# Attention outputs transposed by a crossbar DMA instead of TensorE and VectorE, with the schedule around it shifted

## The chip, the cores and the metric

The kernel runs on one core of one Trainium2 chip. The metric is the time of one execution on the device in microseconds (us), as the median of several runs; most runs of one kernel agree within 0.3%. A profile of one execution gives a page and a trace. Engines are named as the profile names them: PE is TensorE, PEld its weight loads, DVE VectorE, ACT ScalarE, POOL GpSimd, SP the engine that only issues transfers here; SPq is its queue.

## The reference

Two operators follow one another. The first is attention with a hash mask: 4 batches, 8 heads, 768 positions, 64 values per head. A query sees a key only if the signs of six random projections of both agree. The second is a feed-forward block on the 3072 x 512 result: x times w_in (512 x 2048), SiLU, times w_out (2048 x 512).

```python
q_bits = (np.einsum('bhsd,dk->bhsk', q, proj) > 0)      # same for k; bits give a bucket
mask = q_bucket[:, :, :, None] == k_bucket[:, :, None, :]
scores = np.where(mask, scale * np.matmul(q, k.transpose(0, 1, 3, 2)), -1000000000.0)
attn = softmax(scores)                                   # cut
x = np.matmul(attn, v).transpose(0, 2, 1, 3).reshape(B * S, H * D)
h = x @ w_in
out = (h * (1.0 / (1.0 + np.exp(-h)))) @ w_out
```

## The kernel before

Heads are worked in pairs: 16 pairs, four to a batch. A head takes nine windows; a window has one 512-wide score tile (TensorE), its exponential (ScalarE) and four products with v (TensorE). One batch is a stage of 72 windows. While stage b runs, the second operator of batch b-1 is spread through its windows, in units of four 512-column matmuls (or eight of 256). Stage one has no such units; after the last window, the last batch's units run alone.

The attention result of a pair, `x_pr`, has positions on partitions; the first matmul of the second operator needs it transposed, `xT`. Before the change TensorE does it, and VectorE copies the result out of PSUM:

```python
    def x_unit(p):
        xp = ps.tile([P, S], F16, tag="m", name="xt_ps", bufs=3)
        for t in range(NJ):                      # NJ = 6
            nc.tensor.transpose(xp[:, t * P : (t + 1) * P], x_pr[p][:, t, :], ident16)
        xT[p] = xpl.tile([P, S], F16, tag=f"xT{p % 4}", name="xT")
        nc.vector.tensor_copy(out=xT[p], in_=xp)
```

Its first use, one unit of the second operator (four pairs are the four k-tiles, so all four transposes of a batch must be there before the fourth matmul of the first unit):

```python
            for j in range(f):
                ft = grp * f + j
                for dt in range(NDT):            # NDT = 4
                    nc.tensor.matmul(hp[:, j, :], w_in16[dt][:, ft * P : (ft + 1) * P],
                                     xT[4 * b + dt][:, c0 : c0 + n], ...)
```

Everything is placed by window number, and a queue executes in the order of placement. Almost all transfers are issued from one queue (SP), in order; of the large ones only the two weight matrices are loaded from GpSimd's queue, cast to two bytes on the way:

```python
    for dt in range(NDT):
        plan(12 + 6 * dt, lambda dt=dt: load_w_in(dt))
        plan(58 + 5 * dt, lambda dt=dt: load_w_out(dt))     # 4 x 512 KB
    ...
    for Q in range(2, NQUAD):                    # a quad is two pairs, 36 windows
        w0 = (Q - 1) * QST
        ...
            plan(w0 + 1 + i, lambda p=2 * Q + i: load_v(p))
            if Q + 1 < NQUAD:                    # eight loads of 96 KB per pair, 128 B packets
                plan(w0 + (12 if Q == 2 else 21) + i, lambda p=2 * Q + 2 + i: load_blocks(p))
    for p in range(NPAIR):
        plan(2 * NU * (p + 1) + (3 if p % 4 == 3 else 9), lambda p=p: x_unit(p))
    ...
        if w % BST == 1:
            moeq.extend(moe_head())              # units left over by the batch before
        if w % BST == 5 and w > BST:
            moeq.extend(moe_list(w // BST - 1))  # units of the batch that has just ended
```

The softmax here doesn't subtract the row's maximum and nothing guards it: scores larger than these inputs give would overflow.

Of the kernel before, what the change touches and what calls it, by code (L numbers as in the profile page):

```python
# [10 lines left out]
F16 = mybir.dt.float16  # L11
# [6 lines left out]
def kernel(  # L18
# [10 lines left out]
    nc = tc.nc  # L29
    B, H, S, D = q.shape  # L30
# [3 lines left out]
    P = 128  # L34
    NJ = S // P
    NDT = DMODEL // P
    NFT = DFF // P
# [9 lines left out]
    cst = ctx.enter_context(tc.tile_pool(name="cst", bufs=1))  # L47
# [8 lines left out]
    gpl = ctx.enter_context(tc.tile_pool(name="gpl", bufs=1))  # L56
    ops = ctx.enter_context(tc.tile_pool(name="ops", bufs=3))
    ps = ctx.enter_context(tc.tile_pool(name="ps", bufs=1, space=bass.MemoryType.PSUM))
# [31 lines left out]
    def load_v(p):  # L90
        b, h0 = p // 4, 2 * (p % 4)
        t = vld.tile([P, 2, NJ * D], F32, tag="ldv", name="v_sb")
        nc.sync.dma_start(
            out=t, in_=v[b, h0 : h0 + 2].rearrange("h (p t) d -> p h (t d)", p=P))
        v_sb[p] = t
# [18 lines left out]
    ident = cst.tile([P, P], F32, name="ident")  # L114
# [2 lines left out]
    nc.vector.memset(pw, 0.0)  # L117
    nc.gpsimd.dma_start(out=pw[0:64, 0:NBIT], in_=proj)
    nc.gpsimd.dma_start(out=pw[64:128, NBIT + 1 : 2 * NBIT + 1], in_=proj)
    ident16 = cst.tile([P, P], F16, name="ident16")  # L120
    nc.vector.tensor_copy(out=ident16, in_=ident)



# [60 lines left out]
    def block_unit(p, n):  # L185
        if n == 0:
            qk32[p] = t32.tile([P, 2 * S], F32, tag="qk32", name="qk32")

        dst = qk32[p][:, n * S : (n + 1) * S].rearrange(
            "p (t r a) -> p a t r", t=NJ, r=32, a=4)  # L190
        nc.vector.transpose(out=dst, in_=qk_sb[p, "qk"[n]])  # L191
# [96 lines left out]
    NU = 9  # L288
# [24 lines left out]
    x_pr = {}  # L313
# [48 lines left out]
    xT = {}  # L362

    def x_unit(p):
        xp = ps.tile([P, S], F16, tag="m", name="xt_ps", bufs=3)
        for t in range(NJ):
            nc.tensor.transpose(xp[:, t * P : (t + 1) * P], x_pr[p][:, t, :], ident16)  # L367
        xT[p] = xpl.tile([P, S], F16, tag=f"xT{p % 4}", name="xT")
        nc.vector.tensor_copy(out=xT[p], in_=xp)


    after = []
# [1 line left out]
    def flush():  # L374
        for fn in after:
            fn()
        after.clear()

    def moe_units(b):
        g = {}  # L380

        def mm1(ci, grp):
            c0, n, f = ((0, 512, 1), (512, 256, 2))[ci]
            if grp == 0:
                g[ci] = gpl.tile([P, NFT, n], F16, tag=f"g{ci}", name="g")
            hp = ps.tile([P, f, n], F32, tag="m", name="h_ps", bufs=3)
            for j in range(f):
                ft = grp * f + j
                for dt in range(NDT):
                    nc.tensor.matmul(hp[:, j, :], w_in16[dt][:, ft * P : (ft + 1) * P],  # L390
                                     xT[4 * b + dt][:, c0 : c0 + n],
                                     start=(dt == 0), stop=(dt == NDT - 1))
            th = thp.tile([P, f, n], F32, tag="th", name="th")
            nc.scalar.activation(out=th, in_=hp, func=AF.Tanh, scale=0.5)  # L394

            after.append(lambda: nc.vector.scalar_tensor_tensor(  # L396
                out=g[ci][:, grp * f : (grp + 1) * f, :], in0=th, scalar=1.0, in1=hp,
                op0=ALU.add, op1=ALU.mult))

        o2 = {}  # L400

        def mm2_last():

            for i in range(2):
                c = slice(i * DMODEL // 2, (i + 1) * DMODEL // 2)
                op = ps.tile([P, DMODEL // 2], F32, tag="s", name="o2_ps", bufs=3)
                for ft in range(NFT):
                    nc.tensor.matmul(op, g[1][:, ft, P : 2 * P], w_out16[:, ft, c],  # L408
                                     start=(ft == 0), stop=(ft == NFT - 1))
                osb = ops.tile([P, DMODEL // 2], F32, tag="osb", name="osb")  # L410
                nc.vector.tensor_scalar(out=osb, in0=op, scalar1=0.5, scalar2=None,
                                        op0=ALU.mult)
                dst = out[b * S : (b + 1) * S, c].rearrange("(p t) n -> p t n", p=P)
                nc.sync.dma_start(out=dst[:, NJ - 1, :], in_=osb)

        def mm2(tt, part):
            ci, ct = (0, tt) if tt < 4 else (1, tt - 4)
            if part == 0:
                tag = "m" if scoring else "s"
                o2[tt] = ps.tile([P, DMODEL], F32, tag=tag, name="o2_ps", bufs=3)  # L420
            for ft in range(4 * part, 4 * part + 4):
                nc.tensor.matmul(o2[tt], g[ci][:, ft, ct * P : (ct + 1) * P],  # L422
                                 w_out16[:, ft, :],
                                 start=(ft == 0), stop=(ft == NFT - 1))
            if part == 3:
                osb = ops.tile([P, DMODEL], F32, tag="osb", name="osb")
                nc.vector.tensor_scalar(out=osb, in0=o2[tt], scalar1=0.5, scalar2=None,  # L427
                                        op0=ALU.mult)
                dst = out[b * S : (b + 1) * S, :].rearrange("(p t) n -> p t n", p=P)
                nc.sync.dma_start(out=dst[:, tt, :], in_=osb)  # L430

        first = [lambda grp=grp: mm1(0, grp) for grp in range(NFT)]
        second = [lambda grp=grp: mm1(1, grp) for grp in range(NFT // 2)]
        outs = {tt: [lambda tt=tt, part=part: mm2(tt, part) for part in range(4)]
                for tt in range(NJ)}
        if b == B - 1:
            outs[NJ - 1] = [mm2_last]
        return first, second, outs

    def spread(x, y):  # L440

        both = [((i + 0.5) / len(x), 0, u) for i, u in enumerate(x)]
        both += [((i + 0.5) / len(y), 1, u) for i, u in enumerate(y)]
        return [u for _, _, u in sorted(both, key=lambda e: e[:2])]

    late = []

    def moe_head():
        units, late[:4] = late[:4], []
        return units  # L450

    def moe_list(b):


        first, second, outs = moe_units(b)
        units = spread(first, late) + spread(second, sum((outs[t] for t in range(4)), []))
        late[:] = outs[4] + outs[5]
        return units


# [2 lines left out]
    BST = 8 * NU  # L463
    QST = 4 * NU
# [13 lines left out]
    def plan(w, fn):  # L478
        at.setdefault(w, []).append(fn)
# [34 lines left out]
    for Q in range(2, NQUAD):  # L514
        w0 = (Q - 1) * QST
        for i in range(4 if Q > 2 else 0):
            w1 = w0 + (5, 9, 11, 14)[i]
            plan(w1, lambda Q=Q, i=i: block_unit(2 * Q + i // 2, i % 2))
            if i % 2:
                for par in range(2):  # L520
                    plan(w1, lambda p=2 * Q + i // 2, par=par: cast_unit(p, par))
        plan(w0 + 20, lambda Q=Q: proj_unit(2 * Q, 2 * Q + 1))
        for i in range(4):
            plan(w0 + 20,
                 lambda Q=Q, i=i: bits_unit((2 * Q, 2 * Q + 1), i // 2, i % 2))
        for i in range(2):
            plan(w0 + 1 + i, lambda p=2 * Q + i: load_v(p))
            for j in range(2):
                plan(w0 + 18 + 9 * i + 2 * j, lambda p=2 * Q + i, j=j: v_unit(p, (j,)))
            if Q + 1 < NQUAD:  # L530
                plan(w0 + (12 if Q == 2 else 21) + i, lambda p=2 * Q + 2 + i: load_blocks(p))
    for p in range(NPAIR):
        plan(2 * NU * (p + 1) + (3 if p % 4 == 3 else 9),
             lambda p=p: x_unit(p))

    moeq = deque()
# [3 lines left out]
    for w in range(NW):  # L540
        flush()
        for fn in at.pop(w, []):
            fn()
        if w % BST == 1:
            moeq.extend(moe_head())
        if w % BST == 5 and w > BST:
            moeq.extend(moe_list(w // BST - 1))
        keep = 3 if w >= NW - 12 else 0
        left = BST - w % BST
        n = -(-(len(moeq) - keep) // left) if len(moeq) > keep else 0  # L550
        if n == 1 and len(moeq) - keep < left and (w % 3 == 2 or w % QST in (20, 21)):
            n = 0
        for _ in range(n):
            moeq.popleft()()
        av(w)
        if w + LEAD < NW:
            score(w + LEAD)
# [7 lines left out]
    for u in moe_head() + moe_list(B - 1) + late:  # L565
        u()
        flush()
# [28 lines left out]
```

## Time and profile before

| | before |
|---|---|
| time, median of 3 runs | 315.19 us (315.08 to 315.35) |
| span of the profiled run | 313.6 us |
| PE / DVE / ACT busy | 97% / 60% / 68% of the span |
| granted TensorE clock | 1.0 |

The page is read from the chain of waits (its section 4): what ended last, followed back, says which engine sets the end. A group's line (section 5) has busy time and mean length of one, then the idle time of its engine just before it and what ended most of that. A mean length of a matmul is not its price: they overlap, and the price is the distance from start to start.

### The profile page before, as it was taken

What the parts mean: (1) busy time and instruction counts of PE and PEld (TensorE: products, weight loads), DVE (VectorE), ACT (ScalarE), POOL (GpSimd) and SP (SyncE); (2) the same over time, 40 slices, a digit from 0 to 9 for tenths busy, and PEclk for the clock granted to TensorE, in tenths of its full rate; (3) what the DMA queues carried; (4) which work ended last, traced back from release to release, by engine and by line L of the source; (5) the groups of instructions that cost most, each with busy time, mean ns of one, the idle gap of its engine ahead of it and who ended that gap; (6) DMA issues with size and microseconds to landing.
All of it is one profiled execution on the core that took longest, in us unless ns stands there. A gap on an engine that the chain in (4) does not pass through costs nothing.

```text
span 313.6 us, 7308 instructions
## 1 busy us (share of the span) xinstructions
PE 305.5 (97%) x2795; PEld 180.9 (58%) x2795; DVE 186.7 (60%) x372; ACT 212.1 (68%) x389; POOL 124.6 (40%) x197
## 2 busy tenths in 40 slices
PE   6999999999999999999999999999999999999995
PEld 3566665555666565545566566545566665446554
DVE  4788968696559524774658444685533434664341
ACT  2897989998876576878877666786876761553210
POOL 6477999567514831374505750174511110000000
PEclk9999999999999999999999999999999999999999
DMA  7999997980584028800791158500000000001112
GB/s 176 240 254 235 216 148 112 234 139 8 92 136 142 9 45 131 234 7 9 118 201 54 40 81 147 182 2 9 4 36 33 36 33 36 34 0 54 49 58 79
DMA packets 92564, 30.22 MB, mean 96 GB/s; under 512 B 82432, under 2 KB 89072, under 8 KB 92528
## 3 DMA queue, kind: packets, MB, share of 16 engines
q1 hardware_dynamic: 89776, 25.54, 36.9%
q0 software_dynamic: 2752, 4.20, 8.0%
q8 instruction: 22, 0.36, 0.5%
q14 instruction: 14, 0.11, 0.1%
HBM read 27.27 MB, written 6.29 MB: 107 GB/s over the span
## 4 chain that ended last, share of the span: by engine, by line
PE 87%; DVE 6%; ACT 3%; DMA 2%; issue 1%; SPq 0%; ACTq 0%
PE h_ps L390 26%; PE o_ps L422 25%; PE s_ps L306 17%; PE o_ps L338 11%; PE bp_ps L232 3%; ACT u L309 2%; PE tp_ps L177 2%; DMA k_sb<-in_k_dram 2%; PE xt_ps L367 2%; DVE g L396 1%; PE o_ps L408 1%; DVE qk L191 1%; DVE qkb L283 1%; DVE qka L283 1%; DVE qka L255 1%
## 5 line engine op out<-in xcount | busy, mean ns | idle before, releaser
L309 ACT ACTIVATE u<-s_ps 128x512 f16<-128x512 f32 x288 | 156.9, 601 | 45.3 <-PE s_ps L306 44.8
L396 DVE SCALAR_TENSOR_TENSOR g<-th,h_ps 128x512 f16<-128x512 f32 x96 | 65.4, 685 | 84.7 <-ACT th L394 84.5
L390 PE MATMUL h_ps<-xT,win 128*128 128x512 f16 (+1 forms) x512 | 97.1, 326 | 0.6 <-DVE g L396 0.6
L422 PE MATMUL o_ps<-wout,g 128*128 128x512 f16 x368 | 92.2, 379 | 0.0
L338 PEld LDWEIGHTS <-u 128*128 128x128 f16 x1152 | 68.2, 98 | 41.5 <-ACT u L309 9.4
L394 ACT ACTIVATE th<-h_ps 128x512 f32<-128x512 f32 x96 | 57.3, 597 | 39.0 <-PE h_ps L390 36.2
L338 PE MATMUL o_ps<-vv,u 128*128 128x65 f16 x1152 | 82.6, 194 | 0.5
L390 PEld LDWEIGHTS <-win 128*128 128x128 f16 x512 | 49.9, 98 | 32.6 <-issue 1.6
L358 POOL TENSOR_TENSOR x_pr<-osum,rec 128x384 f16<-128x384 f32 x21 | 17.3, 825 | 97.6 <-DVE rec L357 97.2
L422 PEld LDWEIGHTS <-g 128*128 128x128 f16 x368 | 35.4, 98 | 32.6
L306 PE MATMUL s_ps<-qka 71*128 71x512 f16 x192 | 52.7, 327 | 0.6 <-DVE qka L255 0.6
L306 PE MATMUL s_ps<-qkb 128*128 128x512 f16 x192 | 52.7, 326 | 0.0
L199 POOL TENSOR_SCALAR qka<-qk 64x1536 f16<-64x1536 f32 x15 | 21.9, 1463 | 20.0 <-DVE qk L191 12.8
L199 POOL TENSOR_SCALAR qkb<-qk 64x1536 f16<-64x1536 f32 x15 | 22.0, 1468 | 1.2
L427 DVE TENSOR_SCALAR osb<-o_ps 128x512 f32<-128x512 f32 x23 | 15.8, 687 | 9.4 <-PE o_ps L422 9.4
L210 POOL TENSOR_TENSOR vsa<-v_sb 128x192 f32<-128x192 f32 x32 | 19.3, 602 | 0.0
L208 POOL CAST vv<-v_sb 128x384 f16<-128x384 f32 x32 | 16.4, 513 | 3.0 <-DMA v_sb<-in_v_dram 2.8
L306 PEld LDWEIGHTS <-qka 71*128 71x128 f16 x192 | 15.5, 97 | 1.2 <-issue 1.0
L191 DVE STREAM_TRANSPOSE qk<-q_blk 128x768 f32<-128x768 f32 x10 | 15.7, 1573 | 0.0
L191 DVE STREAM_TRANSPOSE qk<-k_blk 128x768 f32<-128x768 f32 x10 | 15.7, 1571 | 0.0
L306 PEld LDWEIGHTS <-qkb 128*128 128x128 f16 x192 | 15.4, 97 | 0.0
L352 DVE TENSOR_TENSOR osum<-o_ps,vsum 128x390 f32<-128x390 f32 x21 | 11.9, 566 | 1.8
(57 smaller groups left out, 184.8 us busy)
## 6 DMA issues: line engine op xcount, KB each, us to landing
v_sb<-in_v_dram SPq DMA_DIRECT2D x16, 384.0 KB
out_dram<-osb SPq DMA_DIRECT2D x23, 256.0 KB
q_blk<-in_q_dram SPq DMA_DIRECT2D x40, 96.0 KB
k_blk<-in_k_dram SPq DMA_DIRECT2D x40, 96.0 KB
q_sb<-in_q_dram SPq DMA_DIRECT2D x6, 384.0 KB
k_sb<-in_k_dram SPq DMA_DIRECT2D x6, 384.0 KB
win<-in_moe_w_in_dram POOLq DMA_DIRECT2D x4, 512.0 KB, 7.5
wout<-in_moe_w_out_dram POOLq DMA_DIRECT2D x4, 512.0 KB, 10.4
```

The source lines that it names most:

```text
L191: nc.vector.transpose(out=dst, in_=qk_sb[p, "qk"[n]])
L199: nc.gpsimd.tensor_scalar(out=dst[rows, :], in0=qk32[p][rows, :], scalar1=CS, scalar2=1.0, op0=ALU.mult, op1=ALU.mult)
L208: nc.gpsimd.tensor_copy(out=vv[:, :, 0:D], in_=src)
L210: nc.gpsimd.tensor_tensor(out=sa, in0=src[:, 0:3], in1=src[:, 3:6], op=ALU.add)
L306: nc.tensor.matmul(sp[:, o0 : o0 + n], t[rows, S + jt * P : S + (jt + 1) * P], t[rows, c0 : c0 + n], start=True, stop=True)
L309: nc.scalar.activation(out=u, in_=sp, func=AF.Exp, scale=ESC)
L338: nc.tensor.matmul(o_ps[h][:, c0 // P + i, :], u[:, o0 + i * P : o0 + (i + 1) * P], vv[:, jt, :], start=(not direct(h) and w % NU == 0 and ...
L358: (nc.vector if direct(h) else nc.gpsimd).tensor_tensor(out=x_pr[p][:, :, par * D : (par + 1) * D], in0=o[:, 0:NJ, 0:D], in1=rec[:, :, Non ...
L390: nc.tensor.matmul(hp[:, j, :], w_in16[dt][:, ft * P : (ft + 1) * P], xT[4 * b + dt][:, c0 : c0 + n], start=(dt == 0), stop=(dt == NDT - 1))
L394: nc.scalar.activation(out=th, in_=hp, func=AF.Tanh, scale=0.5)
L396: after.append(lambda: nc.vector.scalar_tensor_tensor(out=g[ci][:, grp * f : (grp + 1) * f, :], in0=th, scalar=1.0, in1=hp, op0=ALU.add, o ...
L422: nc.tensor.matmul(o2[tt], g[ci][:, ft, ct * P : (ct + 1) * P], w_out16[:, ft, :], start=(ft == 0), stop=(ft == NFT - 1))
```

## The change

Its intent is to take 96 transposes off TensorE, the engine that sets the pace, and 16 copies off VectorE, by one DMA per pair that transposes from SBUF to SBUF. As a DMA lands later than a TensorE transpose is done, the first unit of a batch moves from window 5 to 11 of a stage, and twelve units in place of eight are left over to fill the gap. The diff, without the lines that drop the identity matrix:

```diff
... (identity matrix dropped)
@@ -362,11 +360,9 @@
     xT = {}
 
     def x_unit(p):
-        xp = ps.tile([P, S], F16, tag="m", name="xt_ps", bufs=3)
-        for t in range(NJ):
-            nc.tensor.transpose(xp[:, t * P : (t + 1) * P], x_pr[p][:, t, :], ident16)
         xT[p] = xpl.tile([P, S], F16, tag=f"xT{p % 4}", name="xT")
-        nc.vector.tensor_copy(out=xT[p], in_=xp)
+        nc.sync.dma_start(out=xT[p].rearrange("d (t r) -> d t r", t=NJ),
+                          in_=x_pr[p].rearrange("r t d -> r (t d)"), transpose=True)
 
 
     after = []
@@ -382,7 +378,8 @@
         def mm1(ci, grp):
             c0, n, f = ((0, 512, 1), (512, 256, 2))[ci]
             if grp == 0:
-                g[ci] = gpl.tile([P, NFT, n], F16, tag=f"g{ci}", name="g")
+                g[ci] = gpl.tile([P, NFT, n], F16, tag=f"g{ci}", name="g",
+                                 bufs=2 - ci)
             hp = ps.tile([P, f, n], F32, tag="m", name="h_ps", bufs=3)
             for j in range(f):
                 ft = grp * f + j
@@ -446,15 +443,15 @@
     late = []
 
     def moe_head():
-        units, late[:4] = late[:4], []
+        units, late[:6] = late[:6], []
         return units
 
     def moe_list(b):
 
 
         first, second, outs = moe_units(b)
-        units = spread(first, late) + spread(second, sum((outs[t] for t in range(4)), []))
-        late[:] = outs[4] + outs[5]
+        units = spread(first, late) + spread(second, outs[0] + outs[1] + outs[2])
+        late[:] = outs[3] + outs[4] + outs[5]
         return units
 
 
@@ -524,13 +521,13 @@
             plan(w0 + 20,
                  lambda Q=Q, i=i: bits_unit((2 * Q, 2 * Q + 1), i // 2, i % 2))
         for i in range(2):
-            plan(w0 + 1 + i, lambda p=2 * Q + i: load_v(p))
+            plan(w0 + 5 + i, lambda p=2 * Q + i: load_v(p))
             for j in range(2):
                 plan(w0 + 18 + 9 * i + 2 * j, lambda p=2 * Q + i, j=j: v_unit(p, (j,)))
             if Q + 1 < NQUAD:
                 plan(w0 + (12 if Q == 2 else 21) + i, lambda p=2 * Q + 2 + i: load_blocks(p))
     for p in range(NPAIR):
-        plan(2 * NU * (p + 1) + (3 if p % 4 == 3 else 9),
+        plan(2 * NU * (p + 1) + (2 if p % 4 == 3 else 9),
              lambda p=p: x_unit(p))
 
     moeq = deque()
@@ -543,12 +540,13 @@
             fn()
         if w % BST == 1:
             moeq.extend(moe_head())
-        if w % BST == 5 and w > BST:
+        if w % BST == 11 and w > BST:
             moeq.extend(moe_list(w // BST - 1))
         keep = 3 if w >= NW - 12 else 0
         left = BST - w % BST
         n = -(-(len(moeq) - keep) // left) if len(moeq) > keep else 0
-        if n == 1 and len(moeq) - keep < left and (w % 3 == 2 or w % QST in (20, 21)):
+        skip = w % BST in (0, 2, 5, 7, 10) if w % BST < 11 else w % 3 == 2 or w % QST in (20, 21)
+        if n == 1 and len(moeq) - keep < left and skip:
             n = 0
         for _ in range(n):
             moeq.popleft()()
```

More of the change, by code (lines that the diff above doesn't have):

```diff
@@ L119 @@
     nc.gpsimd.dma_start(out=pw[64:128, NBIT + 1 : 2 * NBIT + 1], in_=proj)
-    ident16 = cst.tile([P, P], F16, name="ident16")
-    nc.vector.tensor_copy(out=ident16, in_=ident)
     NR = 2 * NBIT + 1
```

## The prediction

> **What bounds the kernel now.** I read the page's busy shares first, then its chain of waits, then the groups of instructions, then the timeline of TensorE in three places, and last the DMA share in the stretch where the second stage begins.
>
> The first lines are from the page: busy shares, the chain's shares by engine and by line, and the groups that the change touches (busy time, mean ns of one, idle time before and its releaser).
>
> ```profile
> PE 305.5 (97%) x2795; PEld 180.9 (58%) x2795; DVE 186.7 (60%) x372; ACT 212.1 (68%) x389; POOL 124.6 (40%) x197
> PE 87%; DVE 6%; ACT 3%; DMA 2%; issue 1%; SPq 0%; ACTq 0%
> PE h_ps L390 26%; PE o_ps L422 25%; PE s_ps L306 17%; PE o_ps L338 11%; PE bp_ps L232 3%; ACT u L309 2%; PE tp_ps L177 2%; DMA k_sb<-in_k_dram 2%; PE xt_ps L367 2%; DVE g L396 1%; PE o_ps L408 1%; DVE qk L191 1%; DVE qkb L283 1%; DVE qka L283 1%; DVE qka L255 1%
> L369 DVE COPY xT<-xt_ps 128x768 f16<-128x768 f16 x16 | 8.6, 537 | 4.1 <-PE xt_ps L367 4.1
> L367 PE MATMUL xt_ps<-ident,x_pr 128*128 128x128 f16 x96 | 8.0, 219 | 0.0
> ```
>
> TensorE carries 87% of the chain that ended last, and the transposes that are to go (L367) lie on that chain with 2% of it. VectorE's copy of them (L369) is not among the named parts of the chain, and VectorE as a whole is 60% busy. The busy share of 97% alone proves little, since records of matmuls overlap. So I looked at starts. In the timeline of TensorE at the head of the second stage (start, length, instruction) the units of the second operator and the attention follow without a gap:
>
> ```profile
> 57.67 1.03 PE L390 MATMUL h_ps<-xT,win 128*128 128x512 f16 x4
> 58.53 0.28 PE L338 MATMUL o_ps<-vv,u 128*128 128x65 f16 x4
> 58.65 0.38 PE L306 MATMUL s_ps<-qkb 128*128 128x512 f16 x1
> 58.87 1.03 PE L390 MATMUL h_ps<-xT,win 128*128 128x512 f16 x4
> ```
>
> From start to start: one unit of four 512-column matmuls takes 58.53 - 57.67 = 0.86 us, one window of attention (four products with v, one score) 58.87 - 58.53 = 0.34 us. The chain in order of time shows the last pair's transposes and what follows them:
>
> ```profile
> 261.47 0.34 PE xt_ps L367 x6
> 261.81 3.45 PE o_ps L422 x16
> ```
>
> Six transposes take 0.34 us of the chain, some 56 ns each, not the 219 ns of their record: most of a record is latency that the next matmul hides.
>
> The first batch is different. There no second operator runs yet, and ScalarE's exponentials follow one another:
>
> ```profile
> 31.21 8.76 ACT L309 ACTIVATE u<-s_ps 128x512 f16<-128x512 f32 x17 [1.02 <-PE s_ps L306]
> ```
>
> That is (8.76 - 0.60) / 16 = 0.51 us per window, against 0.34 us of TensorE. So until 57.6 us ScalarE (with some bursts of TensorE and VectorE work) sets the pace, and from there to the end TensorE does.
>
> **What the Trainium skill says.** (1) "VectorE: DVE Perf Modes", The three transpose paths: a full 128x128 transpose costs 390 ns on TensorE and 1309 ns through the DMA crossbar. The trace has 219 ns for TensorE's record and 56 ns for its pitch, so the page's comparison is not the price here; nothing in the trace of before shows a crossbar transpose. (2) "TensorE: Matmul & The Clock Gate", Part 4: PE-mode transpose: the result lands in PSUM and needs a VectorE copy after. The trace agrees: L369, 537 ns per pair. (3) "DMA: Bandwidth & Descriptors", Anatomy of one DMA: about 2.0 us of fixed cost per transfer, mostly the completion. The trace is near: the last output copy ends on VectorE at 310.74 us and the span ends at 313.6 us, 2.8 us for a 128 KB store with its issue. (4) The same page, DMA Transpose (X-bar): two streams that transpose at once can corrupt each other. All sixteen transposes here are issued from one queue, so I expect right results; no run shows it yet.
>
> **The change, part by part.**
>
> Removed from TensorE: 96 transposes. Those of pairs 4 to 15 lie where TensorE is the bound: 12 x 0.34 = 4.0 us off the end. Those of pairs 0 to 3 lie before 57.6 us, in the ScalarE-bound part, worth at most 4 x 0.34 = 1.3 us; I give them 0.5 us (a burst of TensorE work there does starve ScalarE now and then). Sum: 4.5 us.
>
> Removed from VectorE: 16 x 0.54 = 8.6 us, beside TensorE's work; worth nothing directly. One of three PSUM buffers of the shared tag is no longer taken for each transpose, but TensorE waits on that tag hardly at all now (0.6 us before L390), so also nothing.
>
> Added: 16 transfers of 128 x 768 x 2 B = 197 KB from SBUF to SBUF. Estimate: 2.3 us fixed (from the store above, less its issue) plus 768 rows of 256 B; the loads with 256 B packets in this trace moved about 800 such packets per us, so 1 us more, plus up to 1 us to issue: about 4 us each. They are off TensorE; only a late one costs time. For three pairs of every four there are tens of windows of slack. For the fourth of each batch the first matmul of the new batch needs it, and that is why the change moves that start from window 5 to window 11 of a stage and puts six old units ahead of it.
>
> Moved: (a) Stage two (first use of the second operator) has no old units to put ahead. Six windows that had units now have none: TensorE works 0.34 us of ScalarE's 0.51 us in each, 6 x 0.17 = 1.0 us lost, and nothing gives it back, as the rest of the stage is bound by TensorE. (b) In stages three and four six old units fill the gap: 6 x 0.86 + 10 x 0.34 = 8.6 us for the transfer to land. No loss if a transfer takes about 4 us. (c) After the last window three kept units, then six old ones (9 x 0.86 = 7.8 us) run before the last pair is needed. In the queue the last transpose stands behind the store of the output tile that the kept units finish, which is ready after about 3 x 0.86 + 0.3 + 0.7 = 3.6 us; so it has 4.2 us plus the first three matmuls' 0.65 us. With 4 us this is just hidden; I charge 0.3 us. (d) Four more second-matmul units per batch go to the next: the same TensorE work elsewhere, neutral.
>
> One collision. In the table of stretches (PE, PEld, DVE, ACT, POOL busy, clock, DMA share, GB/s) the time when pair 3 is transposed is one when all DMA engines are full with the second weight matrix:
>
> ```profile
> 56.00:60.00 4.00, 4.00 (x47) 2.38 (x45) 2.68 (x3) 3.88 (x9) 2.85 (x6) 1.00 1.17 252
> 60.00:64.00 4.00, 4.00 (x36) 2.21 (x34) 3.42 (x7) 3.88 (x8) 0.94 (x2) 1.00 1.20 234
> ```
>
> Pair 3 is normalised about 10 windows before window 83, 10 x 0.51 = 5.1 us. If its 48 rows per DMA engine alternate with weight packets that take some 98 ns each, that adds 48 x 0.1 = 4.7 us, and 8.7 us against 5.1 us is a TensorE stall of 3.6 us. The change issues the next values (v) after this transpose, which helps. I charge 1.5 us.
>
> Sum: 315.2 - 4.5 + 1.0 + 1.5 + 0.3 = 313.5 us. I lean to 312.5 us, as such offsets look chosen so that the waits just fit, and so the charge for the collision may be too high.
>
> **Rivals.** *All hidden:* the transfers take 3 us or less even beside the weight load; then only the 1.0 us is lost and the time is 315.2 - 4.5 + 1.0 = 311.7 us, or 310.5 if the first four pairs count in full. For it: the queue's own waits are long, 98 us before output stores, so the issuing engine is free, and the DMA share is under 0.5 in most later slices. *The transfer is slow:* six 128x128 blocks at the skill's 1309 ns one after another are 7.9 us, an estimate from that page. Then stage two waits about 3 to 7 us, stages three and four fit just about, and the tail waits about 3 us: 315.2 - 4.5 + 1.0 + 5 + 3 = 319.7 us. For it: nobody has seen one in this trace; against it: the slack in the tail is only 4.8 us and a tuner would have seen it. *ScalarE becomes the bound:* in stages two to four it is busy 49 to 52 of 67 to 70 us, so taking 1.3 us per stage off TensorE leaves TensorE the bound. Unlikely.
>
> **Range and chances.** Two per cent faster is 309.0 us; even with all 16 pairs counted in full and no loss at all, 315.2 - 5.4 = 309.8 us. So faster is nearly excluded: 0.03. Two per cent slower is 321.5 us, which needs over 10 us of new waits, the slow rival and more: 0.06. Within 2%: 0.91. Range for 8 in 10: 309.8 to 316.5 us.
>
> **What would show it.** No L367 or L369, and TensorE's chain share near 87%. A wait of h_ps matmuls for a DMA of xT near 60 us tells the collision; one near 265 us tells the tail. Empty TensorE time between 55 and 61 us tells loss (a). Landing times of the transposes should be near 4 us, longest for pairs 2 and 3. I am wrong if landings exceed 8 us, or if the waits for xT come in every stage, or if the time before 57.6 us changes by over 1.5 us.

## More of the kernel before

One view the prediction did not show, and which the result turns on, is SP's own queue in order of time (start, time spent issuing, what, how many). Before the change, the block loads of pairs 6 and 7 run through it from 28 us on, far ahead of use:

```profile
28.28 7.60 SPq L84 DMA_DIRECT2D q_blk<-in_q_dram  x4
35.98 8.06 SPq L84 DMA_DIRECT2D k_blk<-in_k_dram  x4
44.14 5.89 SPq L84 DMA_DIRECT2D q_blk<-in_q_dram  x4
50.13 2.66 SPq L84 DMA_DIRECT2D k_blk<-in_k_dram  x4
```

Four issues take 2.7 us when nothing holds them, and up to 8 us when the transfers in front do not drain.

## The result, and the profile after

The changed kernel gives right results. It takes 322.88 us (median of 4 runs, 322.51 to 323.57) against 315.13 us (4 runs) for the kernel before: ratio 1.0251, 95% interval 1.0228 to 1.0274. A ratio is the mean time of one kernel's fast runs over that of the other's in the same rounds, so not quite the ratio of the medians. All runs are fast. It is slower by more than 2%, which the prediction gave a chance of 0.06, and outside its range.

From the page of the changed kernel, the busy shares, the slices of granted clock and DMA, the chain by engine and the group of the first matmuls (names as before, line numbers shifted):

```profile
PE 303.2 (95%) x2699; PEld 176.3 (55%) x2699; DVE 180.2 (56%) x355; ACT 212.0 (66%) x389; POOL 124.8 (39%) x197
PEclk9999999958999999999999999999999999999999
DMA  8999999990078415961596138901111203001111
PE 86%; DMA 8%; DVE 2%; ACT 1%; SPq 1%; issue 1%; DVEq 0%; ACTq 0%
L387 PE MATMUL h_ps<-xT,win 128*128 128x512 f16 (+1 forms) x512 | 99.3, 328 | 9.7 <-DMA xT<-x_pr 9.7
```

The 96 transposes are gone, but the first matmuls now wait 9.7 us for a transposed tile, 8% of the chain is DMA, and in the ninth and tenth slice (64 to 80 us) the granted clock is 0.5 and 0.8. TensorE's timeline shows that nearly all of it is one wait, at the first unit of stage two, and a small one in stage three (brackets: idle time before, and what ended it):

```profile
60.34 0.59 PE L387 MATMUL h_ps<-xT,win 128*128 128x512 f16 x2
69.38 1.19 PE L387 MATMUL h_ps<-xT,win 128*128 128x512 f16 x2 [8.45 <-DMA xT<-x_pr]
...
138.46 0.38 PE L387 MATMUL h_ps<-xT,win 128*128 128x512 f16 x1 [1.25 <-DMA xT<-x_pr]
```

Pairs 0 and 1 were there (two matmuls at 60.34 us); pair 2 was not. TensorE works in order: until 69.38 us nothing else runs on it, and the attention behind that matmul stood still too. The table of stretches (busy time of PE, PEld, DVE, ACT, POOL, then clock, DMA share, GB/s) shows the second cost, the clock:

```profile
57.60:62.00 4.40, 3.34 (x34) 1.47 (x35) 3.08 (x5) 3.81 (x8) 1.30 (x2) 1.00 1.39 204
64.00:74.00 10.00, 4.60 (x23) 2.12 (x23) 1.10 (x2) 2.07 (x4) 3.75 (x3) 0.50 0.99 186
```

The clock is at half from 64 to 74 us: for 5.4 of these ten us TensorE stands, and in the other 4.6, after the wait, it works at half pace.

SP's queue tells when the transposes were issued:

```profile
39.05 2.33 SPq L364 DMA_TRANSPOSE xT<-x_pr  x1
41.47 5.21 SPq L84 DMA_DIRECT2D q_blk<-in_q_dram  x4
46.78 2.65 SPq L84 DMA_DIRECT2D k_blk<-in_k_dram  x4
49.53 3.71 SPq L84 DMA_DIRECT2D q_blk<-in_q_dram  x4
53.34 7.76 SPq L84 DMA_DIRECT2D k_blk<-in_k_dram  x4
61.21 6.79 SPq L364 DMA_TRANSPOSE xT<-x_pr  x2
```

Pair 1's transpose waits in the queue for its values until 39 us, and the block loads behind it start at 41.5 us in place of 28.3. Their last four then need 7.8 us to issue, and the transposes of pairs 2 and 3, behind them, start only at 61.2 us, when TensorE is already waiting. Pair 2's values had been ready since 45.2 us (VectorE's last write of them). At that time GpSimd's queue loads the second weight matrix. What that does shows in the table of DMA queues, cut to a stretch (packets, MB, share of 16 engines' time; software_dynamic is GpSimd's queue, hardware_dynamic SP's). First 47 to 53 us in the kernel before, where block loads run alone; then 62 to 66 us in the changed kernel:

```profile
q1 hardware_dynamic: 5304, 0.67, 74.8%
```

```profile
q0 software_dynamic: 739, 0.74, 111.0%
q1 hardware_dynamic: 738, 0.09, 31.3%
```

Alone, SP's small packets go at 5304 / 6 = 884 per us. Beside the weights the DMA engines take one packet of each queue in turn, 739 to 738, and a weight packet (0.74 MB / 739 = 1 KB) is long: SP's packets go at 738 / 4 = 185 per us, a fifth. At these rates a load of 768 packets takes 4 us in place of 0.9 (an estimate), and each waits for those in front.

Whose packets are these? 0.09 MB / 738 is about 120 bytes, so they are still the block loads'; a transpose's have 256 bytes. From 67.8 to 70 us the same table has no line for GpSimd's queue any more, and

```profile
q1 hardware_dynamic: 1226, 0.34, 92.8%
```

that is 0.34 MB / 1226 = 277 bytes a packet: now the transposes run (with a few larger packets of v), after the weights. In this kernel it was therefore not the transposes that took turns with the weights, but the block loads in front of them in the same queue.

### The profile page after: what moved, and what is told of

Read it like the earlier page. It is cut to its first block, busy times and chain, and to the rows that moved or that the text cites. A ratio compares the mean times of both kernels' runs of the same rounds, so it can differ in the third digit from the quotient of the medians.

```text
span 320.7 us, 7156 instructions
## 1 busy us (share of the span) xinstructions
PE 303.2 (95%) x2699; PEld 176.3 (55%) x2699; DVE 180.2 (56%) x355; ACT 212.0 (66%) x389; POOL 124.8 (39%) x197
## 4 chain that ended last, share of the span: by engine, by line
PE 86%; DMA 8%; DVE 2%; ACT 1%; SPq 1%; issue 1%; DVEq 0%; ACTq 0%
PE h_ps L387 26%; PE o_ps L419 25%; PE s_ps L304 17%; PE o_ps L336 10%; DMA xT<-x_pr 3%; PE bp_ps L230 3%; DMA q_blk<-in_q_dram 2%; PE tp_ps L175 2%; DMA k_sb<-in_k_dram 2%; ACT u L307 1%; PE o_ps L405 1%; SPq L84 1%; DVE qka L253 1%; DVE qka L281 1%; PE o_ps L327 1%
## 5 line engine op out<-in xcount | busy, mean ns | idle before, releaser
L387 PE MATMUL h_ps<-xT,win 128*128 128x512 f16 (+1 forms) x512 | 99.3, 328 | 9.7 <-DMA xT<-x_pr 9.7
L304 PE MATMUL s_ps<-qkb 128*128 128x512 f16 x192 | 53.6, 330 | 0.0
L304 PE MATMUL s_ps<-qka 71*128 71x512 f16 x192 | 52.6, 327 | 1.0 <-DVE qka L253 0.6
```

Of the source, the lines that this page charges most:

```text
L304: nc.tensor.matmul(sp[:, o0 : o0 + n], t[rows, S + jt * P : S + (jt + 1) * P], t[rows, c0 : c0 + n], start=True, stop=True)
```

## The experiments

Four theories are told apart. **Q**: the transposes' place in the one in-order queue makes the loss (pair 1's holds back the block loads, and these hold back pairs 2 and 3). **T**: a crossbar transfer is itself slow when it shares the DMA engines with the weight load, its packets alternating with the weights'. **S**: the shifted schedule costs by itself. **C**: the idle stretch costs more than its length, through the clock. Each kernel is the changed one with the edit shown, was correct, and was timed in three rounds (the last in five) beside the kernel before; medians of 4 runs (5 for the last).

| run | time, us | ratio to before | longest wait for xT in the trace, us |
|---|---|---|---|
| changed kernel | 322.88 | 1.025 | 8.45 |
| rebalance_only | 314.84 | 0.999 | no crossbar |
| first4_on_pe | 312.89 | 0.994 | 1.20 |
| act_queue | 325.61 | 1.034 | 4.85 |
| wout_late | 311.24 | 0.988 | 1.29 |
| filler | 320.84 | 1.020 | 1.38, in stage three; 0.85 left at stage two |
| blocks_early | 314.65 | 0.997 | 1.17 |
| wout_late_pair6 | 311.47 | 0.988 | 1.92 |
| before_wout_late | 315.27 | 1.000 | no crossbar |
| pair1_on_pe | 326.12 | 1.036 | 5.20 |
| collide_tail | 316.60 | 1.005 | 3.37 |
| wout_late_blocks12 | 317.94 | 1.006 | none; 7.81 for bits |
| best | 309.98 | 0.9835 | none |

**rebalance_only: the schedule without the crossbar.** `x_unit` is put back as in the kernel before, all other lines of the change stay.

> The changed kernel's schedule (second operator from window 11 on, twelve units left to the next batch, values loaded four windows later, two buffers of g), but all sixteen pairs transposed by TensorE and copied by VectorE as before. Theory Q (the loss comes from the transposes' place in the one DMA queue): the schedule costs the six windows without units at the head of stage two, about 1.0 us, so 316 us, no wait of the h_ps matmuls over 1 us. Theory S (the new schedule itself is what costs): 320 us or more.

314.84 us, ratio 0.9991 (0.9973 to 1.0009). Theory S falls: the later start and the twelve leftover units cost nothing. My own 1.0 us for the six windows without units is not there either.

**first4_on_pe: the first batch back on TensorE.**

```diff
+        if p < 4:    # transposes and copy of the kernel before, then return
```

> The changed kernel, but pairs 0 to 3 transposed by TensorE and VectorE; the other twelve through the crossbar. Theory Q: nothing stands in the queue before the block loads of pairs 6 and 7, these are issued by about 53 us as in the kernel before, no wait for xT and no half clock near 64 us; twelve pairs give 12 x 0.34 = 4.0 us, the later start costs 1.0 us: 312 us. Theory T (crossbar transfers are slow by themselves or beside other traffic): waits for xT of several us remain in stages three, four or the tail, and the time stays above 315 us.

312.89 us, ratio 0.9943 (0.9913 to 0.9973), clock 1.0 in the profiled run. The loss sits in the first four of the sixteen transfers. Two waits remain in stage three, 1.20 and 0.82 us; 314.84 - 4.0 + 2.0 = 312.8 us, so twelve pairs off TensorE giving their 4.0 us agrees with the time.

**act_queue: another issuing queue.**

```diff
-        nc.sync.dma_start(out=xT[p].rearrange("d (t r) -> d t r", t=NJ),
+        nc.scalar.dma_start(out=xT[p].rearrange("d (t r) -> d t r", t=NJ),
```

> The changed kernel with the sixteen crossbar transfers issued from ScalarE's queue in place of the one that issues all loads. Theory Q: block loads are issued by about 53 us as before; the transposes of pairs 2 and 3 are no longer behind them and land in time (wait for xT at the start of stage two under 2 us, no half clock). ScalarE pays about 1.3 us for each issue, 4 x 1.3 = 5 us of them in the first batch where it sets the pace: 313 to 318 us. Theory T: the transfer of pair 3 still meets the weight load and lands late, a wait of over 4 us for xT near 60 us remains.

325.61 us, slower still. The wait at stage two's start is 4.85 us and comes later (73.4 us), and pair 0's issue alone blocked ScalarE:

```profile
28.15 6.50 ACTq L364 DMA_TRANSPOSE xT<-x_pr  x1
```

ScalarE's next exponential starts at 34.75 us: the engine was blocked by its own issue, which took 6.5 us in place of 1.3. A queue of its own does not free the transposes: from 70 to 72 us their packets take turns with the weights', 275 to 275. That speaks for T, but the ScalarE stops disturb the rest of this run.

**wout_late: the weights out of the way.**

```diff
-        plan(58 + 5 * dt, lambda dt=dt: load_w_out(dt))
+        plan(84 + 5 * dt, lambda dt=dt: load_w_out(dt))
```

> The changed kernel with the four loads of the second weight matrix issued 26 windows later (from window 84 in place of 58). Theory Q and theory T both: the block loads and transposes meet no weight traffic between 54 and 68 us; issue of pair 2's transpose by 57 us, wait for xT at most 1 us, no half clock, 312 us. If it stays near 322 us the weights have no part in it and the order of the queue alone makes the wait. If a new wait for wout at the first second matmuls (near 85 us) appears, the load was moved too far.

311.24 us, ratio 0.9877 (0.9862 to 0.9892), clock 1.0. The queue now issues pairs 2 and 3 at 55.7 us in 2.6 us, and stage two starts with no gap:

```profile
52.95 2.66 SPq L84 DMA_DIRECT2D k_blk<-in_k_dram  x4
55.72 2.62 SPq L364 DMA_TRANSPOSE xT<-x_pr  x2
```

```profile
60.11 1.03 PE L387 MATMUL h_ps<-xT,win 128*128 128x512 f16 x4
```

Without the weight load the loss is gone, though pair 1's transpose still stands ahead of the block loads. So the queue's order alone is not enough. The 1.29 us in stage three stays.

**before_wout_late: the control.** The same edit on the kernel before.

> The kernel before with only the second weights loaded 26 windows later: a control for whether the later load gives time of its own. All theories: TensorE sets the pace there and never waits for these weights or for the loads beside them, so 315.0 us, or 1 to 4 us more if the weights come too late for the first second matmul at 82 us.

315.27 us, ratio 0.9998 (0.9983 to 1.0013): the later load gives nothing by itself.

**filler: the clock.** 38 matmuls of constants ahead of the matmul that waits.

```diff
+        if w == BST + 11:
+            fill = ps.tile([P, 512], F32, tag="m", name="fill_ps", bufs=3)
+            for _ in range(38):
+                nc.tensor.matmul(fill, dmat, warm, start=True, stop=True)
```

> The changed kernel with 38 matmuls of constants (38 x 0.216 = 8.2 us of TensorE, result unused) put just ahead of the first matmul of stage two, where TensorE now waits 8.4 us. Theory C (the idle stretch also halves TensorE's clock, for 10 us from 64.0 us on, of which TensorE works some 4.9 us at half pace after the wait): the wait is filled, the clock stays at 1.00, and the time falls by about half of 4.9 us = 2.4 us, to 320.5 us. Rival (the lower clock cost nothing beside the wait): 322.9 us or more.

320.84 us, clock 1.0 in the profiled run; the matmuls fill all but 0.85 and 0.23 us of the wait. 322.88 - 320.84 = 2.0 us is what the half clock cost on top of the wait, with a wide margin: the four runs lie between 320.16 and 323.20 us, so one of them is no faster than the changed kernel. The changed kernel's own trace says 4.6 us at half pace, so 2.3 us. Theory C holds, its size is about 2 us.

**blocks_early: the order of the queue.**

```diff
-                plan(w0 + (12 if Q == 2 else 21) + i, lambda p=2 * Q + 2 + i: load_blocks(p))
+                plan(w0 + (-8 if Q == 2 else 21) + i, lambda p=2 * Q + 2 + i: load_blocks(p))
-                x_pr[p] = xpl.tile([P, NJ, P], F16, tag="xpr", name="x_pr")
+                x_pr[p] = xpl.tile([P, NJ, P], F16, tag="xpr", name="x_pr", bufs=3)
-    upl = ctx.enter_context(tc.tile_pool(name="upl", bufs=6))
+    upl = ctx.enter_context(tc.tile_pool(name="upl", bufs=5))
```

> The changed kernel with the block loads of pairs 6 and 7 planned 20 windows earlier, so that they stand ahead of pair 1's transpose in the queue and not behind it; a third buffer for the transposes' source so that pair 3's does not wait for pair 1's transfer, and one buffer of u less to make room. The weight load stays. Theory Q (what costs is that pair 1's transpose holds back the block loads by 13 us, which then share the DMA engines with the weights, with the transposes of pairs 2 and 3 behind them): blocks issued by about 53 us, transposes of pairs 1 to 3 issued by 58 us, wait for xT at stage two's start under 2 us: 312 to 314 us. Theory T (a transpose beside the weights is slow in itself, its 48 packets per engine alternating with weight packets of 98 ns, 5 to 6 us each): wait of 5 us or more remains, 318 us or more.

314.65 us (312.47 to 315.57, ratio 0.9971, 0.993 to 1.0013). The profiled run, the fastest, has no wait at stage two's start: pairs 1 to 3 are issued from 52.6 us on, and in that run the records of the weights' packets begin only at 60 us, after the transposes. So the two did not meet in that run, and it does not tell Q from T. Its trace shows why: the values (v) now stand behind the moved block loads, GpSimd waits 6.75 us for them and issues the first weights at 58.55 us in place of 52.2. The edit had moved the weights too. The other three runs have mean clocks of 0.988 to 0.993 and are 1.6 to 3.1 us longer. That in them the two met in part is a guess; no trace of them was kept.

**pair1_on_pe: Q in its exact form.** Only pair 1 is transposed by TensorE, so that nothing holds the block loads.

```diff
+        if p == 1:    # transposes and copy of the kernel before, then return
```

> The changed kernel with one transpose of the sixteen, pair 1's, done by TensorE and VectorE; nothing else. Theory Q in its exact form (pair 1's transpose waits in the queue for its values until 39 us and holds back the block loads of pairs 6 and 7 behind it): these loads start to issue some 8 to 10 us earlier and are through by 55 us, the transposes of pairs 2 and 3 issue by 58 us in place of 61 and 65, the wait at stage two's start falls from 8.4 us to under 1.5 us, no half clock; 322.9 - 8 - 2.2 + 0.2 = 313 us. Rival (the transposes as a whole, or the weights alone, make the wait): taking one of sixteen away changes the wait by 1 to 2 us at most, 321 us.

326.12 us, ratio 1.0356 (1.0316 to 1.0396): slower than the changed kernel, the opposite of what Q says. Its first half came true. SP's queue:

```profile
31.92 8.68 SPq L84 DMA_DIRECT2D q_blk<-in_q_dram  x4
40.70 6.04 SPq L84 DMA_DIRECT2D k_blk<-in_k_dram  x4
46.84 3.56 SPq L84 DMA_DIRECT2D q_blk<-in_q_dram  x4
50.50 2.66 SPq L84 DMA_DIRECT2D k_blk<-in_k_dram  x4
53.25 6.78 SPq L372 DMA_TRANSPOSE xT<-x_pr  x2
```

The loads are through by 53.2 us and pair 2 is issued at 53.25, eight us earlier than before. But TensorE then waits twice:

```profile
65.93 0.58 PE L395 MATMUL h_ps<-xT,win 128*128 128x512 f16 x1 [4.56 <-DMA xT<-x_pr]
...
71.71 0.58 PE L395 MATMUL h_ps<-xT,win 128*128 128x512 f16 x1 [5.20 <-DMA xT<-x_pr]
```

From issue to use pair 2 took 65.93 - 53.25 = 12.7 us. In stage three, away from the weights, pair 7 took 138.46 - 135.67 = 2.8 us in the changed kernel (issued at 135.67 us, and TensorE stood waiting for it until 138.46). The DMA queues of this run from 66 to 71 us, when the block loads are long through and only the last transpose is left in SP's queue:

```profile
q0 software_dynamic: 635, 0.63, 88.1%
q1 hardware_dynamic: 658, 0.17, 41.9%
```

Again one for one, and now SP's packets are the transpose's own: 0.17 MB / 658 = 256 B each, at 658 / 5 = 132 per us. So here, other than in the changed kernel, the transposes themselves are slowed by the alternation. Issued earlier they do not escape the weights; the two in a row and the rest of the block loads in front of them meet all of the load. Q in its exact form has fallen. What holds of it is that SP's queue is in order: the transposes also pay for the loads in front.

**collide_tail: the collision by itself.** The wout_late kernel, where the last pair's transpose has no wait, with six loads of the weights' kind into buffers that nobody reads, at the time of that transpose.

```diff
+    def dummy(i):
+        t = ld.tile([P, 3, 512], F16, tag=f"ld{'qk'[i % 2]}", name="dummy")
+        nc.gpsimd.dma_start(out=t, in_=moe_w_out.rearrange("(f p) n -> p f n", p=P)[:, 3 * (i // 2) : 3 * (i // 2) + 3, :])
+
+    for i in range(6):
+        plan(279 + i, lambda i=i: dummy(i))
```

> The run with the second weights loaded later, and six loads of 128 x 1536 elements, cast to two bytes, from the second weight matrix into buffers that nobody reads, issued by GpSimd about 247 us, so that the last pair's transpose (issued at 255.8 us, needed at 259.9 us, no wait now) meets the same kind of traffic that the transposes of pairs 2 and 3 met. Theory T (a transpose's 48 packets per engine alternate with weight packets of about 100 ns): the transfer takes 5 us more, a wait of 3 to 4 us for xT appears near 260 us, time 314 to 315 us. Theory Q alone (only what stands ahead in the same queue matters): no wait, 311.2 us.

316.60 us, 5.4 us more than wout_late. First the two lines of wout_late, issue and first use, then those of collide_tail:

```profile
255.81 1.25 SPq L364 DMA_TRANSPOSE xT<-x_pr  x1
...
259.28 1.03 PE L387 MATMUL h_ps<-xT,win 128*128 128x512 f16 x4
```

```profile
255.60 1.32 SPq L364 DMA_TRANSPOSE xT<-x_pr  x1
...
263.24 0.59 PE L387 MATMUL h_ps<-xT,win 128*128 128x512 f16 x1 [3.37 <-DMA xT<-x_pr]
```

From issue to use 7.6 us, against at most 4.1 us in wout_late (its fourth matmul, 3 x 0.216 us after 259.28 us, did not wait; the same output store stands in front in both). A wait of 3.4 us was expected at 3 to 4. So weight traffic alone makes a transpose late, which Q alone excludes. But packets in turn are the smaller part of it. From 256 to 258 us GpSimd's queue has 419 packets and SP's none, where wout_late had its output store under way from 256 us on. The transpose's own packets come from 260 to 262 us, with only 181 weight packets beside them:

```profile
q1 hardware_dynamic: 753, 0.20, 82.5%
```

They take two us for what took one in wout_late (793 packets from 257 to 258 us). Of some 3.5 us of delay the transpose's own packets thus explain about one; the rest is the store in front, which started late. Why SP's queue got no turn for two us is open.

From 262 us on the clock is at half (mean 0.51 from 262 to 269 us), which I had left out of the expected 314 to 315 us; it makes most of the rest.

**wout_late_pair6 and wout_late_blocks12: the wait in stage three.** In wout_late, with

```diff
-        plan(2 * NU * (p + 1) + (2 if p % 4 == 3 else 9),
+        plan(2 * NU * (p + 1) + (2 if p % 4 == 3 or p in (6, 10) else 9),
```

> The run with the second weights loaded later, and in it the transposes of pairs 6 and 10 planned seven windows earlier, ahead of the sixteen block loads of the next pairs in the queue. Theory Q: the one wait for xT left there (1.29 us at 127.2 us, stage three) comes from these loads, 16 issues of 0.68 us ahead of pairs 6 and 7; it falls below 0.3 us and the time to 310.0 us. Rival (the wait comes from the transfer's own length after pair 7's values are ready): it stays above 1 us, 311.2 us.

311.47 us and a wait of 1.92 us: a miss. Pair 6 went ahead, but the sixteen block loads still stood ahead of pair 7, from 111.15 to 123.06 us, and pair 7 was issued at 123.86 us. The loads themselves have to move:

```diff
-                plan(w0 + (12 if Q == 2 else 21) + i, lambda p=2 * Q + 2 + i: load_blocks(p))
+                plan(w0 + 12 + i, lambda p=2 * Q + 2 + i: load_blocks(p))
```

> The run with the second weights loaded later, and the block loads of all later quads planned nine windows earlier, so that their sixteen issues of 0.68 us (11 us) are over before pair 7's values are ready and do not stand ahead of its transpose. Theory Q: the wait for xT at 127 us in stage three (1.29 us) goes, none comes in its place: 311.2 - 1.3 = 310.0 us. Rival (the wait is the transfer's own length): it stays, 311.2 us.

317.94 us (314.33 to 320.66; the profiled run is slow, being over 1.5% above the fastest; the three fast runs, 314.33 to 318.63, are also slower than wout_late, but have no trace). No wait for xT is left, but a new one came in its place:

```profile
89.26 0.58 PE L304 MATMUL s_ps<-qka 71*128 71x512 f16 x1 [7.81 <-DMA qka<-bits]
```

The block loads of quad 3, now earlier, met the weights, now later; four of them took 7.8 us to issue and the mask bits behind them came late. In that run it is the same collision with other victims.

**best: both moves, kept apart.** wout_late, with the block loads moved from quad 4 on only.

```diff
-                plan(w0 + (12 if Q == 2 else 21) + i, lambda p=2 * Q + 2 + i: load_blocks(p))
+                plan(w0 + (21 if Q == 3 else 12) + i, lambda p=2 * Q + 2 + i: load_blocks(p))
```

> The run with the second weights loaded later, and only the block loads from quad 4 on planned nine windows earlier (those of quad 3 stay, as beside the weights they delayed the bits by 7.8 us in the run before). No transpose meets the weights, and pair 7's does not stand behind sixteen block loads: no wait for xT over 0.3 us anywhere and clock 1.00 throughout; 311.2 - 1.3 = 310.0 us, ratio 0.983 to 0.986 to the kernel before. If a wait for the bits or for xT of over 1 us remains in stage three: 311 us or more.

309.98 us (309.62 to 310.23), ratio 0.9835, interval 0.982 to 0.985: as expected, and faster than both kernels. The chain by engine, and the group of the first matmuls:

```profile
PE 94%; DVE 2%; DMA 1%; ACT 1%; issue 0%; ACTq 0%
L387 PE MATMUL h_ps<-xT,win 128*128 128x512 f16 (+1 forms) x512 | 97.4, 325 | 0.0
```

No idle time is left ahead of them. Against rebalance_only, 314.84 - 309.98 = 4.9 us is what the sixteen crossbar transfers give when none is late, if the moved block loads give nothing by themselves (only the later weights had a control); the transposes' pitch says 96 x 56 ns = 5.4 us.

## Why the prediction was wrong

By its own steps:

- *TensorE is the bound, 56 ns per transpose, 4.5 us off the end*: right. The best run gives 4.9 us, and first4_on_pe the 4.0 us of the twelve later pairs.
- *VectorE's copies and the PSUM buffer are worth nothing*: not tested by themselves; the 4.9 us leave no room for a gain of theirs above the transposes' 5.4 us.
- *(a) Stage two's later start costs 1.0 us*: wrong in size. rebalance_only is 0.3 us faster than before, within its interval of zero.
- *(b) No loss in stages three and four*: wrong for stage three, 1.25 us. I counted the time from the values to the first use, but not the sixteen block loads ahead in the same queue, 11 us of issuing. wout_late_blocks12 and best show it: with the loads moved, the wait is gone.
- *(c) The tail just hides the transfer*: right. No wait there in the changed kernel.
- *(d) Twelve leftover units are neutral*: right, by rebalance_only, which tests (a) and (d) only together.
- *A transfer takes about 4 us*: 2.8 us from issue to use away from the weights (pair 7). The 2.0 us that the prediction takes from the Trainium skill stand in a section on transfers that GpSimd issues; these are issued by SP.
- *A slip in a rival*: 315.2 - 5.4 + 1.0 is 310.8 us, not 310.5. Nothing rests on it.
- *The collision with the weights, charged at 1.5 us*: **this is the step that failed**. The term measured 8.45 us. That packets take turns with the weights' was right (739 to 738). What was wrong is which transfer pays, and when it starts. I let pair 3's transfer begin when its values are ready, set the weights against its own packets alone (worst case 3.6 us), and cut that to 1.5 us because the next values are issued after it; on top I leaned 1.0 us lower because "such offsets look chosen so that the waits just fit". In the changed kernel the block loads in front met the weights and were slowed. Pair 2, ready at 45.2 us, was issued at 61.2 us, when TensorE already wanted it, and its packets ran after the weights. That it took 69.38 - 61.21 = 8.2 us, near the 8.7 us of the prediction, is luck: the sum was made of pair 3's own packets, and this was mostly waiting for block loads. I had counted the weights against one transfer, and not against the whole queue. Moving the loads ahead did not help by itself (pair1_on_pe, 326.12 us), as the transposes then met the weights themselves; parting SP's small packets from the weights did (wout_late, 311.24 us).
- *Left out of the sum*: the half clock after the idle stretch, 2.0 us by the filler. The Trainium skill has it, in "TensorE: Matmul & The Clock Gate", Why this matters for your kernels: no TensorE gaps above about 3 us, else the clock falls back to half. The trace agrees: a gap of 8.45 us from 60.9 us on, and 0.50 from 64 to 74 us. Any long wait on TensorE should be charged with it.

The sum with measured terms: 314.8 (rebalance_only) - 4.9 (transposes) + 9.7 (both waits) + 2.0 (clock) = 321.6 us, against 322.88 us. About 1.2 us stays unassigned. Trace against trace it closes better: the changed kernel's span is 320.7 - 309.5 = 11.2 us longer than wout_late's, of which 8.45 are the wait and 2.3 the half clock in its own trace.

What stays open: pair1_on_pe is 3.2 us slower than the changed kernel, 12.5 us of waits against 9.7, and I did not take apart which packets make the difference. Whether loads that do not cast would slow SP's queue in the same way was not tried. The spread of blocks_early was not looked into with a second trace. In act_queue the stop of ScalarE and the wait for pair 2 or 3 were not separated.

## What to carry to other kernels

A DMA that takes work off the bounding engine has to be placed among the other DMAs, not only on the compute engines: look, in the trace of the kernel before, at what the DMA engines and the issuing queue do in the window where its result is due, and charge the worst case if they are full. A late transfer costs more than its lateness, since an in-order engine stands behind it and TensorE's clock drops. If a good change measures badly, look for the one wait: moving the loads of one matrix from window 58 to 84 turned 2.5% slower into 1.2% faster.

## What the Trainium skill lacked or had wrong

- "DMA: Bandwidth & Descriptors", Rules for kernel authors, says of crossbar transposes: "A transpose next to ordinary DMAs needs nothing". It is said of results, and for these it held: all runs were correct. For time it is not so: beside casting weight loads from another queue, a transpose's packets went one for one with the weights' (635 to 658 in pair1_on_pe), and from issue to use a transpose took 7.6 us in collide_tail, against at most 4.1 us without the loads. That queues share the DMA engines is no gap of the skill; the price for a queue of short packets is.
- The same page has no figure for how long an issue blocks its engine when the DMA engines are busy. Here a crossbar transpose of 128 x 768 two-byte elements took about 1.25 us to issue in a quiet stretch, and 6.5 us on ScalarE's queue beside a weight load.
- "VectorE: DVE Perf Modes", The three transpose paths, gives 390 ns for TensorE and 1309 ns for the crossbar per 128x128 block. In a stream TensorE's cost 56 ns each, and six blocks in one crossbar transfer took 2.8 us with issue and completion, so neither figure sizes this change.
